# A one-core linear-attention block with a squared-ReLU gate: list scheduler, wo folded into the KV block, contraction of 448 as 3 x 128 rows and paired 64-row rests

## The chip, the cores and the metric

The kernel runs on one core of one Trainium2 chip. The metric is the device time of one execution in microseconds (us); lower is better. A number from a profile is a time within the span of one profiled execution (from its first instruction to its last). The device time is usually about 1.7 us longer than the span (185.05 for 183.3 in one look at the kernel before; in c1 and c2 below it is 1.8 to 2.0, and 2.95 in the profiled execution of c2), so spans are compared with spans and times with times.

Engines: TensorE (in the lines PE for matmuls and PEld for weight loads), VectorE (DVE), ScalarE (ACT), GpSimd (POOL) and SyncE (SP), which only issues transfers. L715 means line 715 of that kernel.

## The reference, cut to what matters

```python
xn  = layernorm(x)                                   # x is 2048 x 448, bf16
q, k, v = split(xn @ wqkv)                           # 16 heads of 28
phi = lambda t: where(t > 0, t + 1, exp(t)) + 1e-6
kv  = phi(k)^T v ;  z = sum of phi(k)                # per head, over all 2048 tokens
o   = (phi(q) kv) / (phi(q) z + 1e-6)
s   = o @ wo                                         # 448 x 448
h   = relu(xn @ w1 + b1) ** 2                        # 1792 wide
g   = silu(h @ w2 + b2)
out = x + s * g
```

The sum over tokens in kv and z splits the work: everything up to h can be done group by group (four groups of 512 tokens), and o only after the last group.

## The kernel before

Each engine has a program written by hand in order, with counting semaphores. The names used below: K, V, Q and H are the projections of xn; G is h times w2; S is o times wo. The contraction of 448 is done as four chunks of 112 rows:

```python
def pe_h(g, fi):                                     # H; K, V and Q look the same
    ...
        for c in range(NC_D):                        # NC_D = 4, PD = 112
            last = e.matmul(
                pb[bk][:, 0:512], w_1[:PD, c, fi * 128 : (fi + 1) * 128],
                xoT[:PD, c, g * 512 : (g + 1) * 512], start=(c == 0), stop=(c == NC_D - 1),
            )
```

phi needs one ScalarE and two VectorE operations per tile, with two buffers besides the result: Exp, then max(x, 0) + 1e-6 read from PSUM, then min(exp, 1) + the other. After the last H there follow, in this order: the KV block, the denominators (16 rows of heads), Ln and Exp for 1/den, and then a step repeated 16 times, mixed with G and S:

```python
# RB: 1/den of 16 heads spread to the 112 rows of chunk c (a 16-row contraction)
e.matmul(RBps[w % 2][:PD, 0:512], ehead[:NH, c, :], r16[:NH, ni * 512 : (ni + 1) * 512], start=True, stop=True)
# VectorE: pqT *= RB
# NT: the numerators of chunk c
e.matmul(OBps[w % 2][:PD, 0:512], kvbd[:PD, c, :], pqT[:PD, c, ni * 512 : (ni + 1) * 512], start=True, stop=True)
# ScalarE: copy to xoT ; later S: xoT x w_o, four chunks, per 128 tokens
```

The biases b1 are loaded by a GpSimd transfer, one value per partition and column. All other loads go through one queue: x of group 0 in four pieces, then w_qkv, then the rest.

Of the kernel before, what the change touches and what calls it, by code (L numbers as in the profile page):

```python
# [9 lines left out]
P = 128  # L10
PD = 112
NC_D = 4
DH = 28
NH = 16
HPC = PD // DH


def bass_recurrent_scan__linear_attn_block__dense_activation_squared_relu__prompt_kernel(
    nc: bass.Bass,
    A_x: bass.AP,  # L20
    A_wqkv: bass.AP,
    A_wo: bass.AP,
    B_x: bass.AP,
    B_w1: bass.AP,
    B_b1: bass.AP,
    B_w2: bass.AP,
    B_b2: bass.AP,
    out: bass.AP,
):
    S = A_x.shape[1]  # L30
    D = A_x.shape[2]
    F = B_w1.shape[1]
    assert D == NC_D * PD
    assert S % 512 == 0
    assert F % 128 == 0
    NT = S // 128
    NG = S // 512
    NF = F // 128
    QW = D
    VW = 2 * D  # L40
    NDW = NC_D * NG

    with ExitStack() as es:
        sb = lambda name, shape, dtype: es.enter_context(nc.sbuf_tensor(name, shape, dtype))
        psb = lambda name: es.enter_context(nc.psum_tensor(name, [P, 512], dt.float32))
        sem = lambda name: es.enter_context(nc.semaphore(name))

        ident = sb("ident", [P, P], dt.bfloat16)
        eps5 = sb("eps5", [P, 1], dt.float32)
        eps6 = sb("eps6", [P, 1], dt.float32)  # L50
        mask = sb("hmask", [P, PD], dt.float32)
        mask16 = sb("hmask16", [P, NC_D, NH], dt.float32)
        ehead = sb("ehead", [NH, NC_D, PD], dt.bfloat16)
        x_tok = sb("x_tok", [P, NT, D], dt.bfloat16)
        xn_tok = sb("xn_tok", [P, 4, D], dt.bfloat16)
        xoT = sb("xoT", [P, NC_D, S], dt.bfloat16)
        w_qkv = sb("w_qkv", [P, NC_D, 3 * D], dt.bfloat16)
        w_o = sb("w_o", [P, NC_D, D], dt.bfloat16)
        w_1 = sb("w_1", [P, NC_D, F], dt.bfloat16)
        w_2 = sb("w_2", [P, NF, D], dt.bfloat16)  # L60
        b1f = sb("b1f", [P, NF], dt.float32)
        b2b = sb("b2b", [P, D], dt.bfloat16)
        st6 = sb("st6", [P, NT, 6], dt.float32)
        mv = sb("mv", [P, NT, 2], dt.float32)
        vep = sb("vep", [P, NT], dt.float32)
        rstd = sb("rstd", [P, NT], dt.float32)
        tn1 = sb("tn1", [P, NT], dt.float32)
        tn2 = sb("tn2", [P, NT], dt.float32)
        nmr = sb("nmr", [P, NT], dt.float32)
        actscr = sb("actscr", [P, 1], dt.float32)  # L70
        pqT = sb("pqT", [P, NC_D, S], dt.bfloat16)
        pk_tok = sb("pk_tok", [P, NT, D], dt.bfloat16)
        v_aug = sb("v_aug", [P, NT, NC_D, PD + 1], dt.bfloat16)
        e_q = sb("e_q", [P, 2, 512], dt.bfloat16)
        rt_q = sb("rt_q", [P, 2, 512], dt.bfloat16)
        e_k = sb("e_k", [P, 2, D], dt.bfloat16)
        rt_k = sb("rt_k", [P, 2, D], dt.bfloat16)
        kvbd = sb("kvbd", [P, NC_D, PD], dt.bfloat16)
        zind = sb("zind", [P, NC_D, NH], dt.bfloat16)
        r2hT = sb("r2hT", [P, NF, S], dt.bfloat16)  # L80
        NRB = 6
        ra = sb("ra", [P, NRB, 512], dt.bfloat16)
        outb = sb("outb", [P, 3, D], dt.bfloat16)

        class _Arena:
            def __init__(self, hosts):
                self.slots = []
                for h in hosts:
                    nbytes = mybir.dt.size(h.dtype)
                    for d_ in list(h.shape)[1:]:  # L90
                        nbytes *= d_
                    self.slots.append([nc.lookup_mloc(h).addr, nbytes])

            def alloc(self, name, shape, dtype):
                need = mybir.dt.size(dtype)
                for d_ in shape[1:]:
                    need *= d_
                need = (need + 31) // 32 * 32
                for sl in self.slots:
                    if sl[1] >= need:  # L100
                        handle = nc.alloc_sbuf_tensor_at(name, list(shape), dtype, offset=sl[0])
                        sl[0] += need
                        sl[1] -= need
                        return handle
                return sb(name, list(shape), dtype)

        arena = _Arena([pk_tok, v_aug, w_1, w_qkv])
        NGB = 8
        ln16 = arena.alloc("ln16", [NH, S], dt.float32)
        r16 = arena.alloc("r16", [NH, S], dt.bfloat16)  # L110
        NGG = 8
        gg = arena.alloc("gg8", [P, NGG, D], dt.float32)
        tt = arena.alloc("tt2", [P, 2, D], dt.float32)
        gb = arena.alloc("gb8", [P, NGB, D], dt.bfloat16)
        sgm = arena.alloc("sgm8", [P, NGB, D], dt.bfloat16)

        pb = [psb(f"pb{i}") for i in range(8)]
        tp_bf = [pb[0][:, :].bitcast(dt.bfloat16), pb[1][:, :].bitcast(dt.bfloat16)]

        def tp_out(c, sl):  # L120
            o = (c % 2) * 512 + sl * 128
            return tp_bf[c // 2][:PD, o : o + 128]

        def tp_read(c):
            o = (c % 2) * 512
            return tp_bf[c // 2][:PD, o : o + 512]

        Qps = [pb[2], pb[3]]
        Kps = pb[6]
        Vps = pb[7]  # L130
        KVps = [pb[0], pb[1], pb[2], pb[3]]
        Gps = [pb[0], pb[1]]
        NGD = len(Gps)
        DHps = [pb[4], pb[5], pb[6], pb[7]]
        assert NG <= 4
        RBps = [pb[2], pb[3]]
        OBps = [pb[4], pb[5]]
        Sps = [pb[6], pb[7]]

        s_x0 = [sem(f"s_x0c{j}") for j in range(min(4, NT))]  # L140
        s_x = [sem(f"s_x{g}") for g in range(NG)]
        s_wqkv = sem("s_wqkv")
        s_w1 = sem("s_w1")
        s_w2 = sem("s_w2")
        s_wo = sem("s_wo")
        s_b2 = sem("s_b2")
        s_b1 = sem("s_b1")
        s_out = [sem(f"s_out{si}") for si in range(NT)]
        s_g = sem("s_g")
        sv_bs = sem("sv_bs")  # L150
        sv_nr = sem("sv_nr")
        sv_nrm = sem("sv_nrm")
        sv_xnT = sem("sv_xnT")
        sv_rtk = sem("sv_rtk")
        sv_pk = sem("sv_pk")
        sv_rtq = sem("sv_rtq")
        sv_pq = sem("sv_pq")
        sv_sq = sem("sv_sq")
        sv_kv = sem("sv_kv")
        sv_pqn = sem("sv_pqn")  # L160
        sv_gb = sem("sv_gb")
        sv_t = sem("sv_t")
        sp_gg = sem("sp_gg")
        sp_of = sem("sp_of")
        sv_ofl = sem("sv_ofl")
        sa_xnT = sem("sa_xnT")
        sa_sqrt = sem("sa_sqrt")
        sv_ag0 = sem("sv_ag0")
        sa_ek = sem("sa_ek")
        sa_v = sem("sa_v")  # L170
        sa_eq = sem("sa_eq")
        sa_hr = sem("sa_hr")
        sa_ln = sem("sa_ln")
        sa_ex = sem("sa_ex")
        sa_oc = sem("sa_oc")
        sa_sg = sem("sa_sg")
        st_tp = sem("st_tp")
        st_k = sem("st_k")
        st_v = sem("st_v")
        st_q = sem("st_q")  # L180
        st_h = sem("st_h")
        st_kv = sem("st_kv")
        st_dh = sem("st_dh")
        st_rb = sem("st_rb")
        st_nt = sem("st_nt")
        st_g = sem("st_g")
        st_s = sem("st_s")

        prog = {"sync": [], "act": [], "dve": [], "pool": [], "pe": []}

        def emit(engname, fn):
            prog[engname].append(fn)

        def W(e, s, v):
            if v > 0:
                e.wait_ge(s, v)

        N_SETUP = 0

        x_r = A_x[0].rearrange("(si p) d -> p si d", p=P)  # L200

        def pool_setup(e):
            nonlocal N_SETUP
            n = 0

            def inc(ins):
                nonlocal n
                n += 1
                ins.then_inc(s_g, 1)

            inc(e.memset(ident[:, :], 0.0))
            e.wait_ge(s_g, n)
            inc(e.affine_select(
                out=ident[:, :], in_=ident[:, :], pattern=[[-1, P]], compare_op=ALU.not_equal,
                fill=1.0, base=0, channel_multiplier=1,
            ))
            inc(e.memset(eps5[:, :], 1e-5))
            inc(e.memset(eps6[:, :], 1e-6))
            inc(e.memset(v_aug[:, :, :, PD : PD + 1], 1.0))
            mview = mask[:, :].rearrange("p (b j) -> p b j", b=HPC)  # L220
            inc(e.memset(mask[:, :], 1.0))
            e.wait_ge(s_g, n)
# [58 lines left out]
        def dve_bn(si):  # L281
            def f(e):
                if si < 4:
                    W(e, s_x0[si], 16)
                elif si % 4 == 0:
                    W(e, s_x[si // 4], 16)
# [701 lines left out]
```

## Time and profile before

| | |
|---|---|
| time | 183.68 us, median of 3 (183.58 to 183.89) |
| first K matmul / first H matmul | 11.51 / 21.03 us |
| last H matmul ends / last matmul of all ends | 105.9 / 178 us |
| end of the span | 183.8 us |

The profiled execution is not one of the three timed here: a span of 183.8 us means a time near 185.5. The fast runs of this kernel in the later series have spans of 181.2 to 184.0 us with a median of 182.1, so this profile is 1.7 us longer than the usual run.

The page of the kernel before, part 1 (busy us, share of the span, instructions) and part 4 (the chain of work that ended last, by engine and by line):

```profile
PE 171.7 (93%) x968; PEld 89.5 (49%) x968; DVE 126.0 (69%) x294; ACT 96.8 (53%) x156; POOL 27.2 (15%) x42
...
PE 75%; DMA 10%; DVE 7%; POOL 2%; issue 2%; ACT 1%; POOLq 0%; DVEq 0%; ACTq 0%
```

TensorE bounds the kernel. The windows view of the kernel before, cut at the first H matmul, the end of H and the last matmul; each line has the stretch, its length, the busy time of each engine, the clock and the share of the transfers:

```profile
0.00:21.00 21.00, 18.15 (x152) 13.72 (x153) 12.69 (x29) 11.91 (x20) 5.98 (x27) 1.00 1.01 221
21.00:105.90 84.90, 81.21 (x421) 40.59 (x420) 71.81 (x192) 57.91 (x92) 0.00 (x0) 1.00 0.10 26
105.90:178.00 72.10, 71.66 (x398) 35.04 (x397) 39.02 (x72) 26.36 (x43) 20.95 (x15) 1.00 0.07 23
178.00:183.80 5.80, 0.68 (x4) 0.14 (x2) 2.46 (x4) 0.58 (x1) 0.27 (x1) 0.78 0.12 40
```

TensorE is busy in 81 of 85 us of the groups and all through the stage after H; the tail costs 5.8 us. Pieces of the chain of waits (start, us, what), with two stretches from which spacings are read, and the wait for b1:

```profile
6.19 18.95 DMA b1f<-in_B_b_dram
25.17 0.70 ACT ra L563
...
46.92 7.79 PE pb L549 x36
...
168.45 2.65 PE pb L715 x14
```

A 512-column matmul takes 7.79 / 36 = 0.216 us, a 448-column one 2.65 / 14 = 0.189 us, and a 448-column matmul on a chunk of 112 rows (K: 0.76 us for 4 in the chain) costs as much as one on the 128-row chunks of G. The Trainium skill ("TensorE: Matmul & The Clock Gate", Back-to-back issue gap) gives N / 2.4 GHz + 2.5 ns for the gap of N columns at full clock, which is 0.216 and 0.189 us: this trace agrees. The busy numbers of PE are larger (0.379 us per matmul) because matmuls overlap; that is why spacings are used here.

One step of the stage after H, in the timeline of the kernel before (start, us, engine, line, what, and what ended the idle time before it):

```profile
125.15 0.38 PE L691 MATMUL pb<-pqT,kvbd 112*112 112x512 bf16 x1
...
125.46 0.12 PEld L667 LDWEIGHTS pb<-r_50,ehead 16*112 16x112 bf16 x1 [0.37 <-issue]
125.47 0.42 PE L667 MATMUL pb<-r_50,ehead 16*112 16x512 bf16 x1
125.81 2.38 PEld L715 LDWEIGHTS pb<-w,r2hT 128*128 128x128 bf16 x14 [0.23 <-issue]
125.82 2.82 PE L715 MATMUL pb<-w,r2hT 128*128 128x448 bf16 x14
```

The weight loads of the 16-row matmul and of the one after it start together with their matmuls; elsewhere weight loads run ahead. The step repeats every 125.82 - 122.50 = 3.32 us and holds 14 x 0.189 + 2 x 0.216 = 3.08 us of spacing: 0.24 us go to entering and leaving the 16-row contraction.

### The profile page before, as it was taken

Reading aid. Unit: us, or ns where it says so; the run is one execution under the profiler, and the core shown is the slowest. Engines: PE = TensorE matmul, PEld = TensorE weight load, DVE = VectorE, ACT = ScalarE, POOL = GpSimd, SP = SyncE. Lnnn points to the kernel's source line nnn. Section 1 sums busy time; section 2 is a strip of 40 time slices with the busy share of each in tenths; the row PEclk is TensorE's granted clock in tenths of the full one; section 3 lists DMA queues with packets and bytes.
Section 4 is the critical chain, followed back from the end, with each engine's and each line's share of the span. In section 5 each row is a group of like instructions: output and inputs, shape, how many; then the busy total and the mean of one; then the engine's idle time right before and its main releaser. Section 6 shows DMA issues by size and latency. Waiting matters only on the chain.

```text
span 183.8 us, 2904 instructions
## 1 busy us (share of the span) xinstructions
PE 171.7 (93%) x968; PEld 89.5 (49%) x968; DVE 126.0 (69%) x294; ACT 96.8 (53%) x156; POOL 27.2 (15%) x42
## 2 busy tenths in 40 slices
PE   6979979799998999989999999999999999999980
PEld 6945424455444554445544474444444444434540
DVE  3727959969999699996995440194665556587454
ACT  6447557477784777748778747932332222352120
POOL 7500000000000000000000000000015544468320
PEclk9999999999999999999999999999999999999997
DMA  5999990000000000000000000000000000112101
GB/s 119 258 264 230 253 334 21 0 5 0 0 0 4 0 0 0 2 4 0 0 0 4 2 0 4 0 0 0 0 0 29 27 25 30 45 50 79 50 26 49
DMA packets 9629, 8.78 MB, mean 48 GB/s; under 512 B 2256, under 2 KB 8720, under 8 KB 9616
## 3 DMA queue, kind: packets, MB, share of 16 engines
q1 hardware_dynamic: 7808, 8.60, 17.4%
q0 software_dynamic: 1808, 0.01, 1.4%
q8 instruction: 8, 0.13, 0.3%
q14 instruction: 5, 0.04, 0.1%
HBM read 6.77 MB, written 1.84 MB: 47 GB/s over the span
## 4 chain that ended last, share of the span: by engine, by line
PE 75%; DMA 10%; DVE 7%; POOL 2%; issue 2%; ACT 1%; POOLq 0%; DVEq 0%; ACTq 0%
PE pb L715 24%; PE pb L549 19%; DMA b1f<-in_B_b_dram 10%; PE pb L757 6%; PE pb L468 6%; PE pb L438 5%; PE pb L450 5%; PE pb L667 3%; PE pb L691 2%; PE pb L633 2%; DVE r2hT L573 2%; PE pb L597 2%; DVE xn_tok L342 2%; PE pb L401 1%; ACT ra L563 1%
## 5 line engine op out<-in xcount | busy, mean ns | idle before, releaser
L549 PE MATMUL pb<-xoT,w 112*128 112x512 bf16 x224 | 49.7, 379 | 1.4 <-ACT ra L563 1.4
L563 ACT ACTIVATE ra<-pb,b1f 128x512 bf16<-128x512 f32 x56 | 37.7, 688 | 19.0 <-PE pb L549 14.6
L715 PE MATMUL pb<-w,r2hT 128*128 128x448 bf16 x224 | 45.0, 353 | 0.0
L800 POOL TENSOR_TENSOR outb<-tt_52,x_tok 128x448 bf16<-128x448 f32 x15 | 21.2, 1417 | 149.6 <-DVE tt_52 L788 149.6
L549 PEld LDWEIGHTS pb<-xoT,w 112*128 112x128 bf16 x224 | 21.7, 98 | 27.2 <-issue 1.8
L715 PEld LDWEIGHTS pb<-w,r2hT 128*128 128x128 bf16 x224 | 20.9, 98 | 21.4 <-issue 3.1
L737 ACT ACTIVATE sgm_54<-gb_53 128x448 bf16<-128x448 bf16 x16 | 9.2, 576 | 39.9 <-DVE gb_53 L728 39.9
L573 DVE TENSOR_TENSOR r2hT<-ra 128x512 bf16<-128x512 bf16 x56 | 22.0, 422 | 8.6 <-ACT ra L563 8.6
L728 DVE TENSOR_TENSOR gb_53<-pb,b2b 128x448 bf16<-128x448 f32 x16 | 10.0, 624 | 23.3 <-PE pb L715 23.3
L468 PE MATMUL pb<-xoT,w_qkv 112*112 112x512 bf16 x64 | 16.4, 379 | 0.0
L438 PE MATMUL pb<-w_qkv,xoT 112*128 112x448 bf16 x64 | 14.7, 353 | 1.3 <-DMA w_qkv<-in_A_wqkv_dram 1.3
L450 PE MATMUL pb<-w_qkv,xoT 112*128 112x448 bf16 x64 | 14.7, 352 | 0.0
L757 PE MATMUL pb<-w_o,xoT 112*128 112x448 bf16 x64 | 14.7, 352 | 0.0
L503 DVE TENSOR_SCALAR rt_q<-pb 112x512 bf16<-112x512 f32 x16 | 11.1, 691 | 4.2 <-ACT e_q L487 4.2
L768 DVE TENSOR_TENSOR gg_51<-gb_53,sgm_54 128x448 f32<-128x448 bf16 x16 | 10.0, 624 | 4.7 <-ACT sgm_54 L737 4.6
L788 DVE TENSOR_TENSOR tt_52<-pb,gg_51 128x448 f32<-128x448 f32 x16 | 10.0, 625 | 4.2 <-PE pb L757 3.8
L494 DVE TENSOR_SCALAR rt_k<-pb 128x448 bf16<-128x448 f32 x16 | 10.0, 625 | 3.9 <-ACT e_k L479 3.3
L487 ACT ACTIVATE e_q<-pb 112x512 bf16<-112x512 f32 x16 | 9.6, 597 | 5.1 <-PE pb L468 5.1
L479 ACT ACTIVATE e_k<-pb 128x448 bf16<-128x448 f32 x16 | 8.7, 544 | 4.4 <-PE pb L438 4.4
L517 DVE SCALAR_TENSOR_TENSOR pqT<-e_q,rt_q 112x512 bf16<-112x512 bf16 x16 | 11.0, 685 | 0.0
L699 ACT ACTIVATE xoT<-pb 112x512 bf16<-112x512 f32 x16 | 9.3, 585 | 3.0 <-PE pb L691 3.0
L468 PEld LDWEIGHTS pb<-xoT,w_qkv 112*112 112x112 bf16 x64 | 8.3, 130 | 5.2
(65 smaller groups left out, 153.6 us busy)
## 6 DMA issues: line engine op xcount, KB each, us to landing
w<-in_B_w_dram SPq DMA_DIRECT2D x2, 1568.0 KB, 15.8
out_dram<-outb SPq DMA_DIRECT2D x16, 112.0 KB, 1.7
x_tok<-in_A_x_dram SPq DMA_DIRECT2D x3, 448.0 KB, 17.4
w_qkv<-in_A_wqkv_dram SPq DMA_DIRECT2D x1, 1176.0 KB, 8.8
x_tok<-in_A_x_dram SPq DMA_DIRECT2D x4, 112.0 KB, 2.1
w_o<-in_A_wo_dram SPq DMA_DIRECT2D x1, 392.0 KB, 19.8
b2b<-in_B_b_dram SPq DMA_DIRECT2D x1, 112.0 KB, 13.5
b1f<-in_B_b_dram POOLq DMA_DIRECT2D x1, 7.0 KB, 19.0
```

The lines of the kernel that those rows point to most:

```text
L438: last = e.matmul(Kps[:, 0:D], xoT[:PD, c, si * 128 : (si + 1) * 128], w_qkv[:PD, c, QW : QW + D], start=(c == 0), stop=(c == NC_D - 1),)
L450: last = e.matmul(Vps[:, 0:D], xoT[:PD, c, si * 128 : (si + 1) * 128], w_qkv[:PD, c, VW : VW + D], start=(c == 0), stop=(c == NC_D - 1),)
L468: last = e.matmul(Qps[t % 2][:PD, 0:512], w_qkv[:PD, c, m * PD : (m + 1) * PD], xoT[:PD, c, g * 512 : (g + 1) * 512], start=(c == 0), stop ...
L494: e.tensor_scalar(out=rt_k[:, si % 2, :], in0=Kps[:, 0:D], scalar1=0.0, scalar2=1e-6, op0=ALU.max, op1=ALU.add,).then_inc(sv_rtk, 1)
L503: e.tensor_scalar(out=rt_q[:PD, t % 2, :], in0=Qps[t % 2][:PD, 0:512], scalar1=0.0, scalar2=1e-6, op0=ALU.max, op1=ALU.add,).then_inc(sv_r ...
L517: e.scalar_tensor_tensor(out=pqT[:PD, m, g * 512 : (g + 1) * 512], in0=e_q[:PD, t % 2, :], scalar=1.0, in1=rt_q[:PD, t % 2, :], op0=ALU.mi ...
L549: last = e.matmul(pb[bk][:, 0:512], w_1[:PD, c, fi * 128 : (fi + 1) * 128], xoT[:PD, c, g * 512 : (g + 1) * 512], start=(c == 0), stop=(c ...
L563: e.activation(out=ra[:, u % NRB, :], in_=pb[h_bank(fi)][:, 0:512], func=AF.Relu, bias=b1f[:, fi : fi + 1],).then_inc(sa_hr, 1)
L573: e.tensor_tensor(out=r2hT[:, fi, g * 512 : (g + 1) * 512], in0=ra[:, u % NRB, :], in1=ra[:, u % NRB, :], op=ALU.mult,).then_inc(sv_sq, 1)
L715: last = e.matmul(Gps[si % NGD][:, 0:D], r2hT[:, fi, si * 128 : (si + 1) * 128], w_2[:, fi, :], start=(fi == 0), stop=(fi == NF - 1),)
L757: last = e.matmul(Sps[si % 2][:, 0:D], xoT[:PD, c, si * 128 : (si + 1) * 128], w_o[:PD, c, :], start=(c == 0), stop=(c == NC_D - 1),)
L800: e.tensor_tensor(out=outb[:, si % 3, :], in0=tt[:, si % 2, :], in1=x_tok[:, si, :], op=ALU.add,).then_inc(sm_, 1)
```

## The change

The intent is to give TensorE less to do and to leave it no waits:

1. A small list scheduler takes operations with modelled durations and fixes, before the run, the order of each engine, the PSUM banks and the semaphores. The order on TensorE is given; the other engines take whatever the model says is ready first.
2. wo is folded into the KV block, once per chunk (112 x 448), so S uses phi(q) / den directly and the 16 numerator matmuls with their ScalarE copies vanish.
3. The contraction of 448 becomes three chunks of 128 rows and a rest of 64 rows. The rest of one output uses rows 0 to 63 of the array, that of the next output rows 64 to 127, so that the two may stream together. The last 64 features are loaded and transposed twice for this. Pairs stand alternately at the end and at the start of their block, so that two pairs are often neighbours.
4. phi and the squares work in place; 1/sqrt is one GpSimd power instead of Newton steps on VectorE; the spreading of 1/den is done four groups at once in 32-row tiles, the denominators in four 32-column tiles; b1 is loaded as rows and transposed on TensorE; w_qkv leaves on ScalarE's queue at once; each partition holds 16 consecutive tokens.

The diff is nearly the whole kernel. Its core, cut:

```diff
+def pe_two(a, b, n, mm, reads, first):
     ...
+    lo, hi, full = slice(0, 64), slice(64, 128), slice(0, 128)
+    if first:
+            mm(e, 0, lo, 3, True, False)
+            mm(e, 1, hi, 3, True, False)
+            for c in range(3):
+                last = mm(e, 0, full, c, False, c == 2)
     ...                                    # then the same for output 1
+    else:
+            for w in (0, 1):
+                for c in range(3):
+                    mm(e, w, full, c, c == 0, False)
+            mm(e, 0, lo, 3, False, True)
+            return mm(e, 1, hi, 3, False, True)
     ...
-                e.tensor_scalar(out=rt_k[...], in0=Kps[:, 0:D], scalar1=0.0, scalar2=1e-6, op0=ALU.max, op1=ALU.add)
-                e.scalar_tensor_tensor(out=pk_tok[...], in0=e_k[...], scalar=1.0, in1=rt_k[...], op0=ALU.min, op1=ALU.add)
+                e.tensor_scalar(out=slot, in0=slot, scalar1=1.0, scalar2=1e-6, op0=ALU.min, op1=ALU.add)
+                e.scalar_tensor_tensor(out=slot, in0=ps(buf)[0:rows, 0:n], scalar=1.0 + 1e-6, in1=slot, op0=ALU.add, op1=ALU.max)
     ...
+def fold_wo(c):
+                e.matmul(ps(b)[0:PD, 0:D], kvm[0:PD, c, :], w_o[0:PD, c, :], start=True, stop=True)
+                return e.matmul(ps(b)[0:PD, D : D + 32], kvm[0:KA, c, :], zsel[0:KA, c, :], start=True, stop=True)
     ...
+def spread(c):
+                for g in range(NG):
+                    r = slice(32 * g, 32 * g + 32)
+                    last = e.matmul(ps(bufs[g])[0:PD, 0:512], ehd[r, c, :], rden[r, :], start=True, stop=True)
     ...
-            e.dma_start(w_qkv[:PD, :, :], ...)          # behind the four x tiles of group 0, one queue
+        load_x(0, 1)
+        load_k("act", w_qkv, A_wqkv, "wqkv", 3 * D)     # ScalarE's queue
+        load_x(1, 4)
```

## The prediction

> **What bounds the kernel now.** TensorE. It is busy 172 of 184 us (busy view), and the chain of waits lies 75% on it, 10% on the landing of b1, 7% on VectorE. By spacing inside long runs of the chain, a 512-column matmul takes 0.216 us and a 448-column one 0.189 us. Work by spacing: H 48.4, G 42.4, Q 13.8, K 12.1, V 12.1, S (wo) 12.1, transposes 3.6, KV 3.3, denominators 3.5, spreading 1/den 3.5, numerators 3.5: about 158 us. The rest is the start (first K matmul at 11.5 us, waiting for w_qkv), the tail (last matmul 178, end 183.8) and about 9 us between: the b1 wait near 25 us, VectorE-bound normalisation before the transposes (VectorE is busy 21.4 of 23.5 us in a middle group, windows view), and the switches below.
>
> **Switch cost.** In the timeline a step "14 G, one numerator, one 16-row spread matmul" takes 3.32 us, by spacing 3.08. The weight load around the 16-row matmul is not hidden, as it is elsewhere. I estimate 0.12 us per change of row tile. The Trainium skill ("TensorEngine Tiling", Key Properties) says that changing the tiling mode drains TensorE; the trace agrees in kind.
>
> **What the change does to TensorE work.**
> - Contraction of 448 as 3.5 instead of 4 passes: H -6.0, K and V -3.0, Q -1.7: -10.8 us if a pair really streams together.
> - Pairs stand at the end of one block and the start of the next, so two share a switch in and out. With transposes and KV blocks between some, I count about 32 visits, 0.24 us each plus some lag of the second tile: +9 us. The split so nets only about 2 us.
> - Numerators gone: -3.5. Spreads four at once: -2.4, and 12 of 16 visits saved, -2.9. Denominators in four column tiles: -2.6. Folding wo: +1, its narrow matmuls another +1. S stays 12.1.
> Net TensorE, switches included: about 158 + 4 to about 151.
>
> **Other engines.** VectorE per middle group falls to about 19.7 us: Newton steps go, phi's SBUF half is a one-source bf16 operation (estimate 0.25 instead of 0.62 to 0.69), against about 22 us on TensorE. ScalarE stays near 16.4 us. So TensorE should be the only bound, with 2 to 3 us of stalls in the groups and 1 to 2 us at the hand-over from H to G (last Relu, square, Ln and Exp with two table loads of 1.28 us). The b1 wait goes, since b1 is loaded as rows and transposed. Start: w_qkv leaves first on its own queue but is 15% bigger and shares the engines; first K near 10.5 us. Only 40 warm-up matmuls; an idle gap may cost 1 us of clock. Tail: last S, multiply 0.63, add 0.4, store about 2.6: 4 us, instead of 5.9.
>
> Sum: 10.5 + 151 + 4 + 4 = 169.5; I lean a little on the lag being smaller than feared: **166 us**, range 158 to 174. Chances: faster 0.96, same 0.03, slower 0.01.
>
> **What would show it.** H group spacing per pair of outputs: 7 x 0.216 plus about 0.2 (right) or 8 x 0.216 (no concurrency). Weight loads of the 64-row matmuls exposed. Numerators and their ScalarE copies absent. VectorE busy under 90% in the middle groups. First K at 9.5 to 12 us; b1 out of the chain; tail 4 us.
>
> **What would make it wrong.** Pairs not overlapping (about 8 us slower) or switches free (6 us faster); granted clock falling in the start gap; a static order built from modelled durations that stalls on late DMA, GpSimd's power operation, or PSUM banks.

## The result, and the profile after

The changed kernel takes 171.97 us, median of 4 (170.95 to 172.49), beside 183.78 us (median of 4) for the kernel before. The ratio is 0.9325, 95% interval 0.9268 to 0.9382. Ratios are the mean time of one kernel's fast runs over that of the other's fast runs of the same rounds, so not quite the ratio of the medians quoted. In a second series, on the same chip as experiments a2 to a4, the changed kernel gave 0.9393, so a difference of about 1 us between series is not resolved by the times alone.

Page of the changed kernel, parts 1 and 4:

```profile
PE 155.1 (91%) x913; PEld 74.8 (44%) x913; DVE 102.5 (60%) x246; ACT 76.7 (45%) x130; POOL 24.7 (15%) x42
...
PE 85%; ACT 5%; DMA 4%; DVE 3%; issue 0%; SPq 0%; DVEq 0%
```

The windows view of the changed kernel, with the same four stages (to the first H matmul, H groups, after H, tail):

```profile
0.00:26.70 26.70, 17.00 (x106) 9.91 (x107) 15.54 (x51) 8.27 (x15) 8.24 (x26) 0.87 0.81 270
26.70:107.20 80.50, 80.50 (x493) 36.35 (x494) 55.68 (x144) 53.20 (x94) 2.12 (x2) 1.00 0.00 1
107.20:165.90 58.70, 57.56 (x321) 28.52 (x320) 30.02 (x50) 15.28 (x23) 13.62 (x14) 1.00 0.07 24
165.90:169.70 3.80, 0.00 (x0) 0.00 (x0) 1.24 (x3) 0.00 (x0) 0.70 (x1) 0.96 0.36 121
```

The groups lost 4.4 us although they now also hold the KV block and the folding, the stage after H lost 13.4 us, the tail 2.0. But the start grew by 5.7 us. Counted in the timelines from the first H matmul (21.03 before, 26.58 after), the rest of the span fell from 162.8 to 143.1 us, by 19.7 us; 5.6 us of that were given back before it.

Pieces of the chain of waits of the changed kernel (start, us, what):

```profile
1.23 7.57 DMA x_tok<-in_A_x_dram
...
8.83 1.68 DVE st L412 x3
...
11.27 0.62 PE pb L475 x4
...
12.57 2.93 PE pb L570 x8
...
21.84 1.60 PE pb L570 x8
23.45 3.30 PE pb L590 x16
26.75 4.85 PE pb L604 x24
...
41.91 5.72 PE pb L570 x32
...
112.50 2.76 PE pb L725 x14
115.26 0.36 PE pb L704 x4
115.62 2.75 PE pb L725 x14
```

Three things are to be seen.

First, the pairs work. Twenty-four H matmuls are three pairs of outputs; without concurrency they would take 24 x 0.216 = 5.18 us, with free concurrency 21 x 0.216 = 4.54, and they take 4.85. The 32 K and V matmuls take 5.72, between 6.05 and 5.29. They hold two visits to the 64-row tiling, so a visit, in and out, costs (5.72 - 5.29) / 2 = 0.21 us.

Second, four spreads together cost what one cost. A G with its four spreads repeats every 115.62 - 112.50 = 3.12 us, which is 0.47 more than G alone (2.65). Before, one spread cost 0.216 + 0.24 = 0.46 us. Sixteen of those, 7.3 us, have become four, 1.9 us.

Third, the start is bad. The first block of K and V takes 2.93 us where a later one (the single visit at 21.84) takes 1.60, and it starts at 12.57. VectorE's own timeline in the changed kernel shows why:

```profile
4.02 0.63 DVE L412 BATCH_NORM_STATS2 st<-x_tok 128x6 f32<-128x448 bf16 x1 [4.02 <-DMA x_tok<-in_A_x_dram]
...
4.90 0.15 DVE L420 TENSOR_SCALAR vep<-mv 128x1 f32<-128x1 f32 x1
8.83 1.68 DVE L412 BATCH_NORM_STATS2 st<-x_tok 128x6 f32<-128x448 bf16 x3 [3.77 <-DMA x_tok<-in_A_x_dram]
10.42 0.14 DVE L432 SCALAR_TENSOR_TENSOR nmr<-mv,rstd 128x1 f32<-128x1 f32 x1
```

Tile 0 was ready to be normalised at 6.8 us (its root came from GpSimd then), but the scheduler had put the statistics of tiles 1 to 3 in front. In its model x comes one load after another at 300 GB/s; on the chip the rows of tiles 1 to 3 landed 7.57 us after their issue, beside w_qkv on the other queue. TensorE idled 5.4 us in front of the first transpose, and the block after it ran at half speed: the granted clock was 0.51 between 8.9 and 15.8 us (windows view). The Trainium skill ("TensorE: Matmul & The Clock Gate", Part 1) says that the clock falls to half when TensorE has been idle for a window of about 3.4 us; the spacing of 2.93 us agrees. Two other traces do not fit that length: in b4 and in c3 the clock fell to half after an idle gap of only 2.0 us, and in b1 it held over one of 2.9 us. So from these runs the length of a gap alone does not tell whether the clock is lost.

### The profile page after: what moved, and what is told of

Its sections match the earlier page's. It is cut to its first block, busy times and chain, and to the rows that moved or that the text cites. A ratio compares the mean times of both kernels' runs of the same rounds, so it can differ in the third digit from the quotient of the medians.

```text
span 169.7 us, 2373 instructions
## 1 busy us (share of the span) xinstructions
PE 155.1 (91%) x913; PEld 74.8 (44%) x913; DVE 102.5 (60%) x246; ACT 76.7 (45%) x130; POOL 24.7 (15%) x42
## 3 DMA queue, kind: packets, MB, share of 16 engines
q1 hardware_dynamic: 6028, 7.63, 13.5%
## 4 chain that ended last, share of the span: by engine, by line
PE 85%; ACT 5%; DMA 4%; DVE 3%; issue 0%; SPq 0%; DVEq 0%
PE pb L604 26%; PE pb L725 24%; PE pb L570 14%; PE pb L590 8%; PE pb L749 7%; DMA x_tok<-in_A_x_dram 4%; PE pb L475 2%; PE pb L635 2%; ACT r L615 1%; DVE st L412 1%; PE pb L704 1%; ACT L693 1%; ACT L689 1%; ACT xT L488 1%; ACT pk L547 1%; PE pb L658 1%
## 5 line engine op out<-in xcount | busy, mean ns | idle before, releaser
L604 PE MATMUL pb<-xT,w 128*128 128x512 bf16 (+1 forms) x224 | 47.8, 381 | 0.0
L725 PE MATMUL pb<-w,r 128*128 128x448 bf16 x224 | 44.9, 353 | 0.0
L615 ACT ACTIVATE r<-pb,b1f 128x512 bf16<-128x512 f32 x56 | 35.2, 687 | 18.7 <-PE pb L604 18.7
L763 POOL TENSOR_TENSOR obuf<-obuf,x_tok 128x448 bf16<-128x448 bf16 x14 | 14.3, 1033 | 113.8 <-DVE obuf L758 113.8
L725 PEld LDWEIGHTS pb<-w,r 128*128 128x128 bf16 x224 | 21.5, 98 | 20.9 <-issue 1.3
L623 DVE TENSOR_TENSOR r<-r 128x512 bf16<-128x512 bf16 x56 | 22.9, 420 | 12.6 <-ACT r L615 12.6
L604 PEld LDWEIGHTS pb<-xT,w 128*128 128x128 bf16 (+1 forms) x224 | 17.2, 97 | 26.4 <-issue 10.9
L570 PE MATMUL pb<-w_qkv,xT 128*128 128x448 bf16 (+1 forms) x128 | 25.4, 367 | 2.7 <-ACT xT L488 1.7
L590 PE MATMUL pb<-xT,w_qkv 128*112 128x512 bf16 (+1 forms) x64 | 14.3, 387 | 0.0
L749 PE MATMUL pb<-msb,pqT 112*128 112x448 bf16 x64 | 13.9, 352 | 0.0
```

The source lines that it names most:

```text
L570: return e.matmul(ps((kb, vb)[w])[:, 0:D], xT[rows, c, si * P : (si + 1) * P], w_qkv[rows, c, col : col + D], start=start, stop=stop,)
L590: return e.matmul(ps(bufs[w])[0:PD, 0:512], w_qkv[rows, c, col : col + PD], xT[rows, c, g * 512 : (g + 1) * 512], start=start, stop=stop,)
L604: return e.matmul(ps(bufs[w])[:, 0:512], w_1[rows, c, col : col + P], xT[rows, c, g * 512 : (g + 1) * 512], start=start, stop=stop,)
L615: lambda e, _, fi=fi, slot=slot, buf=bufs[w]: e.activation(out=slot, in_=ps(buf)[:, 0:512], func=AF.Relu, bias=b1f[:, fi : fi + 1]),
L623: return e.tensor_tensor(out=slot, in0=slot, in1=slot, op=ALU.mult)
L725: last = e.matmul(ps(b)[:, 0:D], r2[:, fi, si * P : (si + 1) * P], w_2[:, fi, :], start=(fi == 0), stop=(fi == NF - 1),)
```

## The experiments

All times come with a run of the kernel before on the same chip; a1 to a4, b1 to b4 and c1 to c3 are three series, d1 is a fourth. Where the time from the first H matmul to the end is given, it is the span minus the start of the first piece of H in the chain of waits; for the changed kernel 169.7 - 26.75 = 142.95 us. This number leaves the start out and turned out to be much steadier than the times. Spans are given in tenths, so it is good to about 0.1 us.

### a1: the changed kernel again

> The changed kernel unchanged, as the yardstick of this series and to see its spread: 171 to 172.5 us. Theory: its spread (1.5 us between fast runs) comes from the start, where the first K and V matmuls run at half clock in the profiled run, so the profile should differ from the earlier one in the first 25 us and agree within 0.2 us in every later stage. Rival: the spread is everywhere.

172.54 us, median of 7 (170.71 to 172.99), ratio 0.9393. In the profile H began at 26.04 instead of 26.75, and from there on 142.96 instead of 142.95 us passed. So what varies between these two executions is the start, as expected. The other executions have no profile, so that their spread is of the same origin is likely, not shown.

### a2: no pairs

```diff
-SPLIT64 = True
+SPLIT64 = False
```

> The contraction as 4 x 112 rows, no pairs, nothing else changed. Theory A (from the profile: a pair of outputs takes 1.62 us for H and 1.43 us for K and V where eight full matmuls would take 1.73 and 1.51): the split is worth about 28 x 0.11 + 16 x 0.085 + 8 x 0.08 = 5 us, so about 176.5 us here, less perhaps 1 us because fewer bytes are loaded at the start. Rival (the prediction): the split nets about 2 us, so about 174 us. Rival of the intent: 10.8 us, so 183 us.

176.73 us (174.76 to 178.65), ratio 0.9577; two of its six runs are slow. The fast ones have a median of 176.3, 3.7 us above a1; by the ratios it is 3.4. Its profiled execution is one of its slow runs, so only its stages are used. Its chain of waits, for the same two stretches as above (with its own line numbers):

```profile
45.53 6.05 PE pb L570 x32
...
53.31 5.18 PE pb L604 x24
```

These are exactly 32 x 0.189 and 24 x 0.216. From the first H matmul (29.96) to the end (176.3) it is 146.3 us, 3.4 more than with pairs. That fits the bookkeeping: of 46 pairs from there on, 28 H and 6 Q save 0.216 each and 12 of K and V save 0.189, 9.6 us; 28 visits at 0.21 to 0.24 cost 5.9 to 6.7; 2.9 to 3.7 remain. The net gain lies about midway between the prediction (2 us) and theory A (5), and far from 10.8.

### a3: both rests on the same rows

```diff
-                    mm(e, 1, hi, 3, True, False)
+                    mm(e, 1, lo, 3, True, False)
     ...
-                    return mm(e, 1, hi, 3, False, True)
+                    return mm(e, 1, lo, 3, False, True)
```

> Both 64-row rests of a pair on the same row half (rows 0 to 63), so that the two matmuls cannot stream together; same number of matmuls, same loads, same visits to the 64-row tiling, result still right. If the pairs stream together in the changed kernel: 52 rests are serialised, 28 + 8 of them at 0.216 and 16 at 0.189 us, so about +10.8 us, 182.5 us. If they do not stream together: the same time.

182.48 us (181.7 to 184.39), ratio 0.9958: 9.9 us above a1, expected 10.8. The K and V stretch of the middle group in its chain of waits:

```profile
44.48 6.47 PE pb L570 x32
```

It was 5.72: 0.75 us for four pairs, 0.19 each, one full 448-column matmul. So in the changed kernel the two rests of a pair do stream together. Without that the kernel would stand within 1% of the kernel before, and 6 us above a2 (fast runs), which has no rests at all: the visits would be paid and nothing saved.

### a4: every pair on its own visit

```diff
-            return not flip[0]
+            return False
```

> The 64-row pair always last in its block, so 52 visits to the 64-row tiling instead of 33 (counted in the order of issue); everything else equal. If the cost goes by visit (0.2 us each, theory): about +3.8 us, 175.5 us. If it goes by pair, for instance a lag of the second tile: no change.

176.66 us (175.63 to 180.72, the last one slow), ratio 0.9587; the median of the fast runs, 176.04, is 3.5 us above a1, expected 3.8. Its K and V stretch of the middle group:

```profile
43.63 6.15 PE pb L570 x32
```

Four visits cost 6.15 - 5.29 = 0.86 us, two cost 0.43: 0.21 us per visit, whether one pair or two are inside. The cost goes by visit, not by pair. From the first H matmul on the kernel takes 147.3 us, 4.4 more for 18 more visits, 0.24 each. The page "TensorEngine Tiling (Array Packing)" of the Trainium skill (Key Properties) says that a change of the tiling mode drains TensorE; this run shows what a visit costs, and it fits that, but no run here shows the drain itself.

### b1: longer warm-up

```diff
-        warm(40)
+        warm(135)
```

> Only the number of warm-up matmuls raised from 40 to 135, so that TensorE works on until just before the first transpose. Theory: the first K and V block runs at half clock because TensorE idled 5.4 us; it should take 1.43 instead of 2.93 us, and 1 to 1.5 us of that reach the end: 171 us where the changed kernel shows 172.5. Rival: the clock at the start is worth nothing, because the next block waits for its transposed tile anyway: same time.

172.94 us (172.09 to 174.45): no gain. But the run doesn't test the clock cleanly. The modelled duration of the warm-up grew with it (13.5 us in the model), so the scheduler gave the copy of the first transposed tile to VectorE, behind statistics of later tiles, and the first K matmul came at 15.09 us instead of 12.57 (timeline of b1):

```profile
14.61 0.42 DVE L487 COPY xT<-pb 128x512 bf16<-128x512 bf16 x1
...
15.09 1.60 PE L570 MATMUL pb<-w_qkv,xT 128*128 128x448 bf16 x8 [2.94 <-DVE xT L487]
```

The block then ran at full speed (1.60 in this view, 2.9 in that of the changed kernel). The gain of the clock and the loss of the new order cancel (H began at 27.43 us). The lesson is about such a scheduler: a changed duration reorders other engines. The question of the clock went to c2.

### b2: tile 0 first on VectorE

```diff
-    ... [("x", si)], [("st", si)], 0.553)
+    ... [("x", si)] + ([("xd", 0)] if 0 < si < 4 else []), [("st", si)], 0.553)
```

> Only the place of three instructions on VectorE changed: the statistics of tiles 1 to 3 may not stand before the normalisation of tile 0 (in the changed kernel they do, and wait for x rows that land at 8.1 to 8.8 us, while tile 0 has been there since 4 us). Theory: first transpose near 7.5 us instead of 11.3, first K matmul when w_qkv has landed, about 9 us instead of 12.2; the second tile still waits for the late x rows, near 13.3 us instead of 16.6; about 3 us off, 169.5 us. Rival: w_qkv, not VectorE's order, holds the first matmul, then under 1 us off.

171.55 us (171.31 to 171.62), ratio 0.9325, the same as the first series of the changed kernel and about 1 us better than a1: expected was 3 us off, so this is a miss. The first K matmul did move to 9.20 us as expected, but H began at 26.81, as in the changed kernel. Its chain of waits:

```profile
9.20 2.93 PE pb L570 x8
12.15 0.55 ACT pk L547
12.73 0.28 DVE pk L552
13.01 0.92 DVE xn L441 x3
...
14.65 0.62 PE pb L475 x4
...
15.78 2.91 PE pb L570 x7
```

Two blocks instead of one now ran at half speed, and the other three tiles were normalised as late as before, because their x came late and phi of tile 0 stood in front of them on VectorE. One wait was lifted and the next one held.

### b3: w_qkv behind x, on one queue

```diff
         load_x(0, 1)
-        load_k("act", w_qkv, A_wqkv, "wqkv", 3 * D)
         load_x(1, 4)
+        load_k("sp", w_qkv, A_wqkv, "wqkv", 3 * D)
```

> w_qkv on the same queue as x and behind all four x tiles of group 0 (as in the kernel before), instead of on ScalarE's queue beside them. Theory: x tiles 1 to 3 land near 4.5 us instead of 8.4, nothing on VectorE waits for them any more, w_qkv lands near 10 us, first K matmul there, and the later tiles of group 0 no longer wait: H of group 0 starts near 20.5 us instead of 26, so about 5 us off, 167.5 us. Rival: the separate queue brings w_qkv so much earlier that the order loses: 172 us or more. Also to be read: whether the 1.7 us by which the device time exceeds the span of the profile in every run of the changed kernel (0 in the kernel before) goes away with the second queue.

169.44 us (167.14 to 170.22, two runs slow), ratio 0.9173; the median of the fast runs, 169.07, is 3.5 us below a1's; expected 5. x of tiles 1 to 3 landed 3.3 us after issue instead of 7.6, the first K matmul came at 9.75. Its profiled execution counts as slow against its own fastest, so only its stages are used. Three blocks ran wholly or partly at half speed (2.88, 2.91 and 2.21 us), each tile still waited for its copy, and the first block waited 1.7 us for the b1 rows, whose transpose stands in front of it on TensorE. H began at 25.51. The device time still exceeded the span by 1.7 us, so the second queue is not the reason for that.

### b4: the same with 86 warm-up matmuls

> The same and 86 warm-up matmuls instead of 40, so that the clock is full when w_qkv lands. Theory: another 1 to 1.5 us off against the run before, 166 us. Rival: no change.

169.62 us (168.14 to 170.27), ratio 0.9205: no gain, a miss. The first K and V block came at 10.01 us and did run at full speed (1.60 us), but as in b1 the order changed with the modelled warm-up: the copy of the second tile stood on VectorE behind the statistics of tiles 4 to 7. TensorE waited for it, the clock fell (0.50 from 13.9 us, windows view), and the second block ran at half speed (timeline of b4):

```profile
10.01 1.60 PE L570 MATMUL pb<-w_qkv,xT 128*128 128x448 bf16 x8
...
13.93 2.91 PE L570 MATMUL pb<-w_qkv,xT 64*128 64x448 bf16 x8 [1.99 <-DVE xT L487]
```

H began at 25.14 us, 0.4 us before b3's. So the longer warm-up did not remove the stretch at half speed; it moved it behind the next gap.

In b1 to b4 the time from the first H matmul to the end was 142.96 to 142.99 us, as in the changed kernel. Whatever one does to the start stays in the start.

### c1: the folding undone

The KV block is kept with K on the rows (the operands of its matmul exchanged), the 16 numerators and their copies come back, S uses w_o:

```diff
+        def num(c):
+            for g in range(NG):
+                ... e.matmul(ps(b)[0:PD, 0:512], kvm[0:PD, c, :], pqT[0:PD, c, g * 512 : (g + 1) * 512], start=True, stop=True)
+                ... e.activation(out=xT[0:PD, c, g * 512 : (g + 1) * 512], in_=ps(b)[0:PD, 0:512], func=AF.Copy)
     ...
-                        ps(b)[:, 0:D], pqT[0:PD, c, si * P : (si + 1) * P], msb[0:PD, c, 0:D], start=(c == 0),
+                        ps(b)[:, 0:D], xT[0:PD, c, si * P : (si + 1) * P], w_o[0:PD, c, 0:D], start=(c == 0),
     ...                                     # fold_wo not called; num(c) after the G that follows spread(c)
```

> The folding of wo undone inside the changed kernel: the KV block is kept as it is, 16 numerator matmuls (0.216 us each) and 16 ScalarE copies come back, the output projection again uses wo; the scheduler, the pairs and the four-at-once spreads stay. Theory: + 3.5 us for the numerators, - 0.95 us for the folding (103.05 to 103.99 us in the chain of the changed kernel), perhaps + 0.5 us of waits for banks: 2.5 to 3.5 us more than the changed kernel, about 175 to 176 us. Rival: the fold is worth most of the 11.8 us that the stage after H lost, then 180 us or more.

175.33 us (173.68 to 175.78), ratio 0.9545: 2.8 us above a1, as expected. From the first H matmul on it took 171.7 - 26.15 = 145.55 us, 2.6 more than with the folding. Its chain of waits shows the numerators at their plain spacing:

```profile
110.90 2.76 PE pb L755 x14
113.65 0.86 PE pb L735 x4
```

The folding is worth what its matmuls are worth (16 x 0.216 - 0.94), and no more.

### c2: the start put right

On top of b3: the statistics of tiles 1 to 3 behind the normalisation of tile 0, those of tiles 4 to 7 behind the last transposed tile of group 0; the late GpSimd constants behind the roots of group 0; the transpose of b1 behind the K and V blocks; 60 warm-up matmuls before and 40 after the first transpose; the transposes one tile ahead; each spread one G later.

```diff
-    ... [("x", si)], [("st", si)], 0.553)
+    ... [("x", si)] + ([("xd", 0)] if 0 < si < 4 else [("xT", 3)] if 4 <= si < 8 else []), [("st", si)], 0.553)
     ...
-            pool(lambda e, _: e.memset(va[:, :, :, PD:KA], 1.0), [("va1",)], dur=0.6)
+            pool(lambda e, _: e.memset(va[:, :, :, PD:KA], 1.0), [("va1",)], [("rstd", 1)], dur=0.6)
     ...
-        gg(0)
-        spread(0)
         gg(1)
+        spread(0)
```

> A version meant to beat both: w_qkv behind the x tiles on one queue; on VectorE the statistics of tiles 1 to 3 behind the normalisation of tile 0 and those of tiles 4 to 7 behind the last transposed tile of group 0; on GpSimd the late constants behind the two reciprocal roots of group 0; the b1 transpose out of the way of the first K and V block; warm-up kept on until w_qkv lands; the spreads one G later. Theory: the start of the changed kernel is bound by the order on VectorE and GpSimd, one wait behind the other (lifting one alone gave 0 to 3 us); with all lifted K and V start near 9.5 us at full clock and H of group 0 near 19.5 us instead of 25.1 to 26.8, and the hand-over loses its 1.1 us: 163.5 us. Rival: a further wait takes its place and it stays near 168 us.

164.06 us (163.62 to 165.75), ratio 0.8936 (0.8896 to 0.8976); expected 163.5. The output is right. It beats both kernels. The profiled execution is the longest of its six (165.75). Its chain of waits, and the first window:

```profile
8.19 2.23 PE pb L786 x40
10.43 1.43 PE pb L569 x8
...
12.71 1.60 PE pb L569 x8
...
14.54 2.86 PE pb L569 x16
...
17.51 3.43 PE pb L589 x16
20.94 4.85 PE pb L603 x24
```

```profile
0.00:20.90 20.90, 19.01 (x166) 13.61 (x167) 13.13 (x39) 7.08 (x13) 7.70 (x25) 1.00 0.94 308
```

The first block takes 1.43 us instead of 2.93, and H begins 5.8 us earlier than in the changed kernel. From there on it takes 162.8 - 20.94 = 141.9 us, 1.1 less than the others: the wait of the first spread for 1/den is gone (in the changed kernel TensorE waits 1.1 us there for ScalarE's last Exp).

### c3: the kernel before, one look

> The kernel before, one look: to read its span beside the device time of the same execution. In all runs of the changed kernel the device time is 1.7 us above the span of the profile. If that is so here too, spans and times can be compared; if it is 0 here, 1.7 us of the change lie outside the span.

185.05 us for a span of 183.3: the same 1.7 us. There is no sign that any of the change lies outside the span; the 0 in b3's expectation had compared the span of one execution with the times of others. (The profile shown of the kernel before has a span of 183.8, so it is not of the fastest executions; that is why the spans differ by 14.1 us and the times by 11.8.)

This second profile shows one more thing. In the kernel before, the wait for b1 lies behind the first H matmul, and here it cost clock as well: TensorE idled 2.0 us, the granted clock was 0.50 between 26.5 and 28 us (windows view), and the 28 H matmuls after the wait took 7.89 us in the chain, where 28 x 0.216 is 6.05. From the first H matmul (19.78) to the end it took 163.5 us, against 162.8 in the first profile. So this number is steady in the changed kernel but not in the kernel before, and neither profile is of a typical fast execution.

### d1: phi as before

```diff
-  e.tensor_scalar(out=slot, in0=slot, scalar1=1.0, scalar2=1e-6, op0=ALU.min, op1=ALU.add)
-  e.scalar_tensor_tensor(out=slot, in0=ps(buf)[0:rows, 0:n], scalar=1.0 + 1e-6, in1=slot, op0=ALU.add, op1=ALU.max)
+  e.tensor_scalar(out=rt, in0=ps(buf)[0:rows, 0:n], scalar1=0.0, scalar2=1e-6, op0=ALU.max, op1=ALU.add)
+  e.scalar_tensor_tensor(out=slot, in0=slot, scalar=1.0, in1=rt, op0=ALU.min, op1=ALU.add)
```

> phi as in the kernel before (Exp, then a max-and-add from PSUM, then a min-and-add of two bf16 tiles, 0.62 to 0.69 us each) inside the changed kernel; all else the same. VectorE gets about 0.35 us more for each of 32 tiles, 2.8 us per group, on 14 to 16.4 busy of 22.4 us. Theory: TensorE alone bounds the middle groups, so their 22.3 us from Q to Q stay within 0.1 us, and only the start, where VectorE's order binds, may lose up to 1 us: 172.5 to 173.5 us. Rival: VectorE's load was part of the gain in the groups, then each group takes 1 us or more longer and the time is 176 us or more.

171.82 us (171.3 to 172.88), ratio 0.9338: no loss. VectorE was busy 112.4 us instead of 102.5, and 18.1 of 22 us in each of two middle windows (the third busy time of the line):

```profile
39.00:61.00 22.00, 21.79 (x135) 9.93 (x134) 18.12 (x47) 14.07 (x26) 1.45 (x1) 1.00 0.00 1
```

The time from the first H matmul on was again 170.6 - 27.64 = 142.96 us. The lighter phi is off the critical path; even with VectorE at 18 of 22 us its work costs nothing here.

## Why the prediction was right or wrong

The time, 171.97 us, lies in the predicted range (158 to 174), and the chance of "faster" was rightly placed. The point, 166, was 6 us too low. The predicted sum was 10.5 + 151 + 4 + 4 = 169.5 us for the span, which is 169.7; but that agreement is chance, as the terms show. For the stretch from first K to first H the prediction's own spacings give 10.2 us: four pairs of K and V (4 x 7 x 0.189 = 5.3), Q (14 x 0.216 = 3.0), 12 transposes (0.056 each, 0.7) and five visits at 0.24 (1.2).

| term | predicted, us | measured in the trace, us |
|---|---|---|
| first K matmul | 10.5 | 12.57 |
| lost from first K to first H (clock, waits for tiles) | 0 to 1 | 26.75 - 12.57 - 10.2 = 4.0 |
| TensorE's work with its switches | 151 | 169.7 less the other terms = 148.2 |
| waits in groups and at the hand-over | 4 | 1.1 |
| tail after the last matmul | 4 | 3.8 |

Of the 4.0 us, 1.3 are the first block at half speed (2.93 against 1.60) and 2.1 are waits for copied tiles (1.09, 0.52 and 0.52 in the timeline); the rest was not taken apart.

- **What bounds it, and the removed matmuls: right.** TensorE carries 85% of the chain. Spreads (7.3 to 1.9 us) and denominators (about 3.6 to 1.0 us: 16 matmuls in 3.62 us before, 0.98 in the chain of c2) are gone as priced (5.3 and 2.6). The numerators are gone too; the folding that pays for them cost 0.94 us and not 2, so they net 2.6 us (c1) and not 1.5.
- **Pairs stream together, but the gain is mostly paid back in switches: right in mechanism, mis-sized.** "The split so nets only about 2 us": 3.4 us in a2 from the first H on. The term that was too big is "0.24 us each plus some lag of the second tile: +9 us". A visit costs 0.21 to 0.24 us and the lag is nothing that a4 could see, so 33 visits cost 7 to 8 us.
- **VectorE off the critical path: right.** It was predicted at 19.7 of about 22 us in a middle group and measured at 16.4 of 22.3 and 14.0 of 22.5; d1 shows that it does not matter even at 18. The feared stalls of 2 to 3 us in the groups did not come: the waits view shows none there.
- **Hand-over and tail: right.** 1.1 us (predicted 1 to 2) and 3.8 us (predicted 4). b1 is out of the chain.
- **The start: wrong, and this is the step that failed.** "first K near 10.5 us", and "an idle gap may cost 1 us of clock": it was 12.57, outside the 9.5 to 12 us that were to show it, and 4.0 us more were lost behind it. The prediction looked at when w_qkv would land. What held TensorE were the instructions of VectorE, standing in an order made from modelled durations, behind x rows that landed late because w_qkv shared the engines. It was listed under what could make the prediction wrong, but was given no time. Against the kernel before it cost 5.6 us up to the first H matmul; c2 got 5.8 us of it back.
- **Leaning down from 169.5 to 166 was a mistake.** The lag was smaller, as hoped, but the start ate that, and the 1.7 us between span and device time was not counted.

The 19.7 us won after the first H matmul are made up of: pairs 3.4 (a2), folding 2.6 (c1), spreads 5.4 and denominators 2.6 (spacings), tail 2.0, and waits of TensorE from 4.1 to 1.1 us (before: 2.3 for normalised tiles, 1.4 behind the b1 wait, 0.4 for the z columns). That is 19.0; the rest was not pursued. The 19.7 us themselves lean on one profile of the kernel before that is 1.7 us longer than its usual fast run, so a part of them, up to about that size, may belong to that execution and not to the change. The kernel before was not changed part by part, so for spreads, denominators, tail and waits this is a reading of two traces, not an experiment.

Open: why b3, with x early and the first K at 9.75 us, still needed until 25.51 us for H was read from its chain and removed together with other waits in c2; c2 does not say what each of its parts is worth alone. A clean test of the clock alone failed (b1, b4), so the half clock is seen, but what it costs by itself is not shown. How much of the spread of single runs comes from the start was seen in two profiles only.

## What to carry to other kernels

Row-tiled rests pay by the visit, not by the matmul: here entering and leaving the 64-row tiling costs about as much as one 512-column matmul, so a pair alone gains next to nothing and two neighbouring pairs gain half of what they promise; count the visits before splitting a contraction. A static order made from modelled durations is only as good as the model where transfers are late: look first at the in-order engines around the first matmuls, because an instruction that waits for a load holds back all behind it that had their data, and lift the waits together, since lifting one only shows the next. To compare variants of a kernel whose start jitters, take the time from a fixed event in the middle (here the first H matmul) to the end: it repeated within 0.1 us in seven profiles of the changed kernel and of variants that alter only its start or its phi, where times spread over 2 us.

## What the Trainium skill lacked or had wrong

- "TensorEngine Tiling (Array Packing)", Key Properties, says that changing the mode drains TensorE and gives no figure. Here a visit to the 64-row tiling cost 0.21 us by the spacing of K and V (a4 against the changed kernel) and 0.24 us over all (4.4 us for 18 visits); the 16-row step of the kernel before gave 0.24 us.
- "TensorE: Matmul & The Clock Gate", Part 3, models the time of packed tiles as that of one matmul plus 4 ns per further tile. For rests mixed into full-array work this leaves out the visit, which here is as long as the matmul itself (0.21 beside 0.216 us). Inside a visit no lag of the second tile was seen, which agrees with the page.
- The same page, Back-to-back issue gap, gives about 131 ns per matmul for a sustained stream of weight loads and 512-column matmuls. Here 36 of them took 0.216 us each (chain of the kernel before), which is what the page calls the isolated gap.
- The same page, Part 1, warns that clock events of a trace may be unreliable. Here they were incomplete: a2's profile records a mean clock of 0.995, while its first three K and V blocks took 3.17 to 3.18 us each instead of 1.51. The first clock event of its trace stands at 24.2 us, behind these blocks, and the views count the time before it as full clock. The spacing of matmuls is the better record. Its idle window of about 3.4 us does not fit every gap seen here: the clock fell after 2.0 us of idle time in b4 and c3 and held over 2.9 us in b1.
- No page gives the time of GpSimd's power operation, which stands in the start of the changed kernel: 0.56 us for 128 x 1 and 1.01 us for 128 x 4 elements (f32, timeline; spans on GpSimd are rough).
